# One transfer for w_out, paired quarters of w3, a bounded load queue and a new order in a fused attention and FFN kernel

## The chip, the cores and the metric

The kernel runs on one core of one Trainium2 chip. The core has five engines with an instruction queue each: PE (TensorE, matmuls and their weight loads), DVE (VectorE), ACT (ScalarE), POOL (GpSimd) and SP (SyncE, which here only issues transfers), and 16 DMA engines that they share. The metric is device time in microseconds (us), the median of several runs.

## The reference

The first part is linear attention with a polynomial sketch, in 4 batches of 4 heads with 1088 rows of 32; the second a multiplicative FFN on 4352 tokens of 128. q, k and v are float32. S1, S2 (8×32) and the FFN's weights arrive as float64.

```python
phi(x) = einsum(S1 x, S2 x) -> 64 features per row      # a_i * b_j
kv  = einsum('bhsf,bhsd->bhfd', phi(k), v);  z = sum(phi(k), over s)
num = einsum('bhsf,bhfd->bhsd', phi(q), kv)
den = einsum('bhsf,bhf->bhs', phi(q), z) + 1e-6
x   = (num / den) as (B*S, H*D) = (4352, 128)
a, b = x @ w1, x @ w2                                    # 128 x 1024 each
out = ((a * b) @ w3) @ w_out                             # 1024 x 1024, 1024 x 128
```

## The kernel before

**Weights.** float64 words come in as raw 8-byte integers and are made float32 on the chip. There are eleven chunks of 1 MB, `w0` to `w10`: w0 and w1 are the two column halves of w1 and w2, `w2` is the matrix w_out, `w3` to `w10` are eight blocks of 128 rows of the matrix w3. (A step's name `w3` is a chunk, not the matrix.) Chunk n has the steps `.load` (SP issues its transfers, L306 to L315), `.load2` (ACT's queue issues the rest, L328), `.c`, `.m` and `.s` (three passes on ACT, L343, L351, L347) and `.j`, `.a` (two on DVE, L362, L367). The buffer `raw` exists three times. Chunks 2 to 10 are loaded in quarters of 32 partitions (L317 to L324): quarters 0 and 2 from SP, 1 and 3 from ACT's queue. A chunk of w3 puts a quarter of the columns on each group of 32 partitions, four row blocks side by side.

**Fold.** w3 and w_out are multiplied beforehand into w3o. For block ko, `f{ko}.t` (L395) transposes the 32×32 squares of the chunk on DVE, `f{ko}.m` (L401) does eight matmuls against `wo`, and `f{ko}.o` (L405) copies the result to `w3o` on ACT. The partition on which a row of w_out lies fixes the order in which the transposes have to read the chunk.

**Attention.** Steps `k{b}.…`, `kr{m}.…`, `v{b}.…` and `kh{b}.…` load k and v and build the products with phi(k) for batch b. `.max`, `.lead`, `.rest` and `.l16` split k in parts, `.gram` (L516) multiplies them on PE, `.Gm` to `.Gb`, `.Ta`, `.Na` shape the results on DVE, `.kT`, `.ab`, `.abt` and `.kp` form phi(k), `.kv0` to `.kv3` and `.kvr` (L616, L623) multiply with v, `.kvm` (L630) masks them, `.kz`, `.ky` and `.kw` hold what q needs. Steps `q0` to `q7` take 512 rows of each of four heads, `qr` the 256 remaining tokens. `q0.A0`, `q0.C0`, `q0.A1`, `q0.C1` are its sketch matmuls, `.al`, `.phi` and the steps beginning with `s` make its features on DVE, `.pt0` and `.pt1` transpose them on PE (L1079), `.x` (L1098) multiplies with kv, `.xs` (L1104) divides on DVE, `.xT` copies the FFN's input on ACT. From q2 on the division is in `.pv` (L1072) and the input is made by `.xT0` to `.xT3` (L1140).

**FFN.** There are nine token groups, `g0` to `g7` with 512 columns and `gr` with 256. For each of eight column blocks c of the weights, `a` (L1182) and `b` (L1192) are matmuls into one of three PSUM buffers `h`, `c` (L1187) copies a on ACT, `m` (L1198) multiplies on DVE, and `o` (L1206; L1210 for gr) adds the product with w3o to the output. `.oT` transposes the output on DVE (L1219) and `.st` stores it by SP.

**Order.** Every piece of work is a named step. One list, ORDER (L36 to L95), names them all in the order in which they are put down, and the end of the kernel ties each instruction to the one before it on its engine (L1255 to L1259). So each engine does its steps in the order of that list, and a step that waits holds all that come later on its engine, transfers on SP included. The steps `warm0` to `warm9` are matmuls on zeros whose result isn't used (L181); WARM gives how many each does, 32 in all.

Of the kernel before, what the change touches and what calls it, by code (L numbers as in the profile page):

```python
# [25 lines left out]
WARM = [11, 3, 2, 5, 1, 1, 4, 1, 2, 2]  # L26

BY_PE = ()
QUEUE2 = "act"

# [6 lines left out]
c.zeros c.ident k0.zero k0.load0 k0.loadr k0.load1 v0.zero q0.load s.zero c.act s.load w0.load w1.load k0.max0  # L37
k0.max1 k0.nat0 k0.nat1 k0.g0 k0.g1 k0.lead0 warm0 k0.tr1 k0.lead1 k0.l160 k0.rest0 s.words k0.tr0 k0.rest1
k0.kT1 k0.gram0 k0.l161 s.pair q0.tr s.split k0.gram1 q1.tr s.lead w0.c s.P k0.Gm q0.restT k0.Gt q0.max k0.kT0
k1.zero k1.loadr k1.load kr0.load k0.Gr c.mask s.T w0.m w0.j k0.Ga s.blk kh1.load s.Pp q0.l2 warm1 k0.ab1 q0.l1  # L40
k0.abc1 v0.loadr k0.Gb warm2 k0.T0 w0.s q0.rm k0.kp1a k0.T1 k0.ab0 v0.load k0.Ta w3.load w1.c k1.max w2.load
k0.kp1b w3.load2 s.blkh k0.Tb warm3 q0.A0 q0.C0 k1.g w1.s w0.a k1.lead k0.N0 k0.Ts q0.sma k1.rest warm4 k0.N1
k1.kT1 kr0.tr kr0.kT k0.abc0 q0.sta warm5 kr0.ab q1.max k1.l16 k0.Na w1.m q0.sha warm6 k1.gram0 k0.kp0a k0.Nb
q0.sla k1.gram1 k1.kT0 w2.load2 k0.Nf k0.Nl k0.Nh warm7 q0.C1 w1.j kr0.abc q1.l2 kr0.kp q0.A1 q0.sca k0.kv0
q0.C1t w3.c k0.kv3 q0.smy q0.al k0.kv2 k0.kp0b q0.sty k1.gram2 q0.phi q1.l1 k2.zero k2.loadr warm8 k0.kv1 q1.rm
k2.load k0.kvr q0.pt0 w4.load w4.load2 q0.shy q0.pt1 k0.kvm q0.pc0 q0.sly k0.kzt k1.Gm kr1.load q0.scy k1.ab
q0.pc1 q0.p01 q0.p2 k0.kz w2.c k0.kw q0.p12 q1.A0 w1.a q0.x q1.load w2.m q0.dn k1.abt q1.C0 w2.s q0.de q1.sm
k1.kp1 q0.rc k1.Gt q0.xs w3.s k2.max q0.xt k0.kyt q0.xT q1.st k0.ky warm9 g0.0a w2.j w3.m w3.j g0.0b k2.g g0.0c
w2.a g0.3a w4.c g0.0m kr1.tr g0.1a g0.3c q1.sh kr1.kT k2.lead g0.3b g0.1c w4.s w4.j g0.1b k2.rest g0.3m g0.2a
q1.sl g0.1m g0.2b k1.Ga q1.scy k1.Gr g0.6a v1.zero v1.load v1.loadr w6.load w5.load w5.load2 g0.2c k2.l16 q1.sca  # L50
k1.Gb g0.5a w4.m g0.2m w3.a kr1.ab g0.5b g0.6c w7.load kr1.abc w4.a g0.5c k2.gram0 w7.load2 k2.gram1 q1.al g0.5m
k1.T0 w6.load2 k2.gram2 f0.t k1.T1 g0.6b k3.zero k3.loadr w5.m k1.kp0 kh2.load g0.7a g0.6m w5.c f1.t g0.4a g0.7c
k3.load f0.m q1.p01 g0.4c q1.p2 w5.s k2.Gm q1.p12 k1.Ta q1.dn g0.7b f0.o w5.j w6.c f1.m k1.Tb q1.de w5.a w7.c
q1.rc g0.0o g0.7m f1.o w6.m k1.Ts q1.bs g0.4b w6.j q1.phi w7.s g0.1o w10.load k1.kv0 w8.load f2.t w6.s k1.kv2
k1.kv1 k1.kv3 k1.kvr q1.pt0 w7.j w8.load2 q1.pt1 w6.a f2.m q1.pc0 q1.pc1 k1.kw f3.t w7.m q1.x g0.4m f2.o
w10.load2 w9.load f3.m w7.a q1.xT w8.c q2.tr k3.max g1.1a f3.o w8.m k1.N0 g1.1b k2.Gt f4.t g1.1c g0.3o w10.c
k2.kT1 k1.N1 g1.7a g1.1m q2.max g1.7b g1.7c k1.Na w9.load2 f4.m g1.7m w8.s w8.j k1.Nb g1.5a w10.j q2.l2 k1.Nf
f4.o w8.a g1.5b q2.l1 g1.5c g1.4a k1.Nl g1.5m k1.kyt f5.t g1.4c g1.4b w10.s g1.6a g1.4m g1.0a k1.ky k2.Gr g1.6c
k3.g k2.Ga k3.lead w9.m g1.6b k2.kT0 f5.m k3.l16 k1.Nh q2.rm k2.Gb w10.m k3.rest k2.ab g1.0c q2.C0 k2.abt w9.c
w10.a k2.kp0 k3.gram0 q2.A0 q3.tr k3.gram1 q1.restT k2.T0 k2.T1 g1.0b g1.6m k2.Ta g0.4o q3.max kr1.kp g0.2o  # L60
g1.0m k2.kp1 q3.l2 f7.t f5.o g1.2a q3.l1 w9.s g1.3a q2.At k2.Tb v2.zero v2.load q2.load kh3.load v2.loadr g1.2b
q3.rm g1.3c q2.Ct g1.2c k2.kv0 w9.j k3.gram2 q4.tr k2.kv1 k2.kv2 q3.C0 w9.a k2.Ts q2.sm k2.kv3 q3.A0 f6.t k2.kvr
f7.m v3.zero q2.st q4.max f6.m k3.Gm q4.l2 k3.kT0 f7.o g1.2m q4.l1 k2.kw q2.sh g0.5o k3.kT1 f6.o k2.N0 k2.N1
g0.6o k2.Na q2.sl g0.7o k2.Nb q2.scy q2.sca g1.3b g0.oT q2.al k3.ab g0.st q2.p01 q2.p2 g1.3m g1.0o q2.p12 k3.Gt
q2.dn g1.6o q3.At q2.de k3.Gr v3.load g1.4o q2.rc k3.Ga q2.bs k3.abt g1.1o q2.phi v3.loadr g1.3o q3.Ct k2.kyt
g1.2o q2.pv k2.ky g1.5o k3.Gb q4.rm q2.x k3.kp0 g1.7o q2.xT0 q2.xT3 q2.xT2 q3.sm q2.xT1 g2.2a q3.st q5.tr g2.2b
k3.kp1 g2.2c g2.0a g2.2m g2.7a q3.sh g2.0c q3.sl g2.0b g1.oT g2.7c q3.sca g1.st g2.7b q3.scy q3.al g2.0m g2.3b
k2.Nf q3.p01 q5.max g2.3a k2.Nh g2.7m k3.kv0 g2.3c q3.p2 k3.kv1 k2.Nl k3.kv3 g2.3m q4.A0 k3.kv2 q4.C0 q3.p12
q4.At q3.dn q3.de q5.l2 k3.kvr q3.rc g2.0o q3.bs q3.phi g2.1a q2.restT g2.6a q3.pv q3.load g2.1c q5.l1 g2.6b
k3.kw g2.6c g2.2o g2.6m q4.Ct g2.1b q5.rm q3.x q3.restT q4.sm q4.st g2.6o q3.xT0 q4.sh q3.xT3 g2.1m g2.5a g2.5b  # L70
g2.5c q3.xT2 q3.xT1 g2.1o g2.5m q5.A0 q5.C0 k3.T0 k3.T1 g3.5a k3.Ta k3.Tb g2.5o g3.5c k3.Ts q4.sl g3.5b qr.max
q5.At q5.sm g2.4a g3.5m g2.4b q4.scy g2.4c g3.0a g2.4m q4.sca g3.6a q7.tr q6.tr g2.3o g3.6c g3.0c g3.2a g3.6b
g3.0b g3.6m q4.al g2.4o g3.2c q4.p01 g3.0m qr.l2 g3.4a qr.l1 qr.rm g2.7o g3.4c k3.N0 g2.oT k3.N1 g3.2b q4.p2
g2.st g3.4b g3.2m q6.max g3.3a k3.Na g3.3b g3.3c q4.p12 q5.st q4.dn g3.0o q4.de q4.rc g3.4m g3.6o g3.3m g3.1b
q4.bs q4.phi g3.3o g3.1a k3.Nb k3.Nl q5.Ct g3.7a q4.pv k3.kyt g3.7c g3.2o k3.ky g3.1c q4.x g3.1m g3.5o q5.sh
q4.xT0 q4.xT3 q4.xT2 q5.sl q4.xT1 k3.Nh q5.scy g4.2a k3.Nf q5.sca g3.7b qr.A0 g3.7m qr.C0 q5.p01 g4.2b g4.2c
qr.At q5.al q6.l2 qr.sm q5.p2 g3.4o q5.p12 q5.dn g4.0a g4.2m g4.0b g4.0c g4.1a g4.0m qr.st g4.7a g4.1c q6.l1
g4.1b g4.7c g3.1o g4.1m q6.rm g4.3a q5.de q5.rc g4.7b g4.3c q5.bs q5.phi g4.5a g3.7o q5.pv g4.5b qr.Ct qr.sh
g4.7m q5.x q7.max g4.3b q5.xT0 q5.xT3 q5.xT1 g4.5c q6.A0 q5.xT2 q6.C0 g4.5m qr.sl g4.3m g5.0a qr.sca qr.al
qr.scy qr.p01 q6.At g4.4a g5.0c q6.sm qr.p2 g5.0b g3.oT g4.4c qr.p12 q7.l2 q6.st g3.st g4.0o g5.0m q7.l1 g4.4b  # L80
g4.6a g4.4m qr.dn g5.4a qr.de qr.rc q6.sh g4.5o g5.4c q6.sl qr.bs g4.6c q6.Ct g4.3o q7.rm g5.4b qr.phi g5.6a
g5.4m q6.sca g4.1o g5.6c g5.6b g4.4o g5.6m q6.scy g4.6b g5.5a g4.6m q6.al g5.5b q6.p01 g5.5c q6.p2 q6.p12 g5.1a
q6.dn qr.pv g5.3a q6.de q6.rc g5.5m qr.x g5.3c g5.1c g5.3b g5.7a g5.3m q6.bs g4.2o g5.7c q6.phi qr.xT0 qr.xT2
g4.6o qr.xT1 q7.C0 q7.A0 g4.7o q7.Ct g5.1b g4.oT q7.At g5.2a g4.st q7.sm g5.2b q7.st g5.1m g5.0o q6.pv g5.2c
qr.xT3 g5.4o q7.sh q6.x q7.sl g5.2m q7.scy g5.7b q7.sca q6.xT0 q6.xT3 q6.xT1 q6.xT2 g5.2o g5.7m q7.p01 g5.3o
q7.al q7.p2 g6.7a q7.p12 q7.dn g6.4a g6.7c g5.1o g6.4c g6.7b g6.4b g6.7m g5.6o g6.4m g6.6a g6.2a g6.6c g6.2b
g6.2c g6.6b g6.2m q7.de g6.3a g6.6m q7.rc g6.3b g6.3c q7.bs g6.5a g6.3m q7.phi g5.5o g6.0a q7.pv g5.7o g6.0c
g6.5c g6.5b g6.0b q7.x g6.0m g5.oT gr.3a q7.xT0 q7.xT2 g6.5m g5.st g6.0o gr.3c q7.xT3 q7.xT1 g6.1a g6.1b g6.1c
gr.3b g6.1m g7.0a gr.3m g6.2o g7.0c g7.1b g7.1a g6.6o g7.1c g7.1m g6.3o g7.0b g7.7b g7.0m g7.7a g6.4o g7.7c
g7.7m g6.5o g6.1o g7.4a g6.7o g7.4c g7.5a g6.oT g7.4b g6.st g7.5c g7.0o g7.4m g7.5b g7.2a g7.5m g7.2b g7.2c  # L90
g7.3a g7.2m g7.1o g7.3c g7.6b g7.6a g7.3b g7.6c g7.6m g7.4o g7.3m gr.5a gr.5b gr.5c g7.2o gr.5m gr.4a gr.4b
gr.4c g7.5o gr.4m gr.2a g7.3o gr.2c gr.2b g7.6o gr.2m g7.7o gr.0a g7.oT gr.0b gr.0c gr.1a g7.st gr.0m gr.7a
gr.1c gr.0o gr.7c gr.1b gr.3o gr.1m gr.2o gr.6b gr.6a gr.4o gr.6c gr.7b gr.6m gr.5o gr.7m gr.1o gr.6o gr.7o
gr.oT gr.st
"""  # L95


def bview(t, free):
    return bass.AP(tensor=t.tensor, offset=t.offset, ap=[list(t.ap[0])] + [list(d) for d in free])


def make_steps(ctx, tc, q, k, v, S1, S2, moe_w1, moe_w2, moe_w3, moe_w_out, out):
    nc = tc.nc
    dve, act, pe, pool, sp = nc.vector, nc.scalar, nc.tensor, nc.gpsimd, nc.sync
    B, H, S, D = q.shape
# [196 lines left out]
    def conv(n):  # L302
# [3 lines left out]
        def _():  # L306
            raw[n] = sb("raw", [128, 1024], I64)
            if n < 2:
                for i, w in enumerate((moe_w1, moe_w2)):
                    sp.dma_start(raw[n][:, i * 512:(i + 1) * 512], w[:, n * 512:(n + 1) * 512])  # L310
            elif n - 3 in BY_PE:
                sp.dma_start(raw[n], moe_w3[(n - 3) * 128:(n - 2) * 128])
            else:
                quarter(sp, 0)
# [975 lines left out]
```

## Time and profile before

| | |
|---|---|
| median of 5 runs | 276.0 us (273.41 to 276.7) |
| profiled execution | 276.1 us, span 274.3 us |
| granted TensorE clock, mean | 0.994 |
| PE busy | 256.3 us, 93% |
| DVE busy | 187.5 us, 68% |
| ACT busy | 110.8 us, 40% |
| POOL busy | 27.1 us, 10% |
| DMA | 22.52 MB, mean 82 GB/s |

Times inside the profile count from the start of the span; the execution's own time is 1.8 us longer. "L516" is line 516 of the kernel. PE's busy time overlaps its weight loads (PEld), and the rows of a timeline overlap too, since an instruction begins before the one ahead has left the pipeline. In a row of a group stand the line, the engine, the operation, what it writes and reads with the shape, how often, the busy us and mean ns of one, and the idle time of the engine just before. A wait is put down to what came last. "issue" is time in which an engine waited for nothing that the profile shows. The chain of work that ended last is followed back from the last instruction.

### The profile page before, as it was taken

Reading aid. Unit: us, or ns where it says so; the run is one execution under the profiler, and the core shown is the slowest. Engines: PE = TensorE matmul, PEld = TensorE weight load, DVE = VectorE, ACT = ScalarE, POOL = GpSimd, SP = SyncE. Lnnn points to the kernel's source line nnn. Section 1 sums busy time; section 2 is a strip of 40 time slices with the busy share of each in tenths; the row PEclk is TensorE's granted clock in tenths of the full one; section 3 lists DMA queues with packets and bytes.
Section 4 is the critical chain, followed back from the end, with each engine's and each line's share of the span. In section 5 each row is a group of like instructions: output and inputs, shape, how many; then the busy total and the mean of one; then the engine's idle time right before and its main releaser. Section 6 shows DMA issues by size and latency. Waiting matters only on the chain.

```text
span 274.3 us, 5772 instructions
## 1 busy us (share of the span) xinstructions
PE 256.3 (93%) x2341; PEld 140.7 (51%) x2341; DVE 187.5 (68%) x434; ACT 110.8 (40%) x192; POOL 27.1 (10%) x51
## 2 busy tenths in 40 slices
PE   8787399997979989999999999999999999999994
PEld 3574185574643758445454444444454444444574
DVE  4788389996959997999945786687658555223321
ACT  4765269768469652023322313334132123212121
POOL 2637022320000430000000000000000000000000
PEclk9999889999999999999999999999999999999999
DMA  7789879799982050502200200002002001102020
GB/s 210 266 217 235 180 187 246 174 229 202 221 162 70 9 160 2 110 12 41 84 1 1 38 2 2 0 2 38 0 2 39 2 0 19 20 2 38 0 37 21
DMA packets 32170, 22.52 MB, mean 82 GB/s; under 512 B 21392, under 2 KB 26640, under 8 KB 32144
## 3 DMA queue, kind: packets, MB, share of 16 engines
q1 hardware_dynamic: 28752, 16.92, 26.8%
q10 hardware_dynamic: 3392, 5.24, 8.7%
q8 instruction: 18, 0.29, 0.5%
q14 instruction: 8, 0.07, 0.1%
HBM read 19.93 MB, written 2.23 MB: 81 GB/s over the span
## 4 chain that ended last, share of the span: by engine, by line
PE 72%; DMA 11%; ACT 6%; DVE 3%; issue 3%; SPq 2%; POOL 1%; ACTq 1%; DVEq 0%
PE a_ps L1182 20%; PE ps_o L1206 20%; PE b_ps L1192 19%; DMA raw<-in_moe_w_dram 6%; DMA kh<-in_k_dram 3%; PE ps_c L862 3%; PE ps_xb L1126 2%; PE ps_w3o L401 2%; ACT sg L347 2%; ACT sg L351 2%; PE ps_o L1210 1%; PE ps_kv L616 1%; DMA kk<-in_k_dram 1%; PE ps_g L516 1%; ACT cv_c L343 1%
## 5 line engine op out<-in xcount | busy, mean ns | idle before, releaser
L1198 DVE TENSOR_TENSOR ab<-ffa,b_ps 128x512 f32<-128x512 f32 (+1 forms) x72 | 46.6, 650 | 53.5 <-PE b_ps L1192 35.8
L1187 ACT COPY ffa<-a_ps 128x512 f32<-128x512 f32 (+1 forms) x72 | 39.9, 561 | 95.7 <-PE a_ps L1182 83.3
L1192 PE MATMUL b_ps<-xT,w 128*128 128x512 f32 (+1 forms) x144 | 69.4, 574 | 0.0
L1182 PE MATMUL a_ps<-xT,w 128*128 128x512 f32 (+1 forms) x144 | 68.5, 575 | 0.4 <-ACT ffa L1187 0.3
L1206 PE MATMUL ps_o<-ab,w3o 128*128 128x512 f32 x128 | 63.8, 600 | 3.1 <-ACT w3o L405 3.1
L1182 PEld LDWEIGHTS a_ps<-xT,w 128*128 128x128 f32 x144 | 26.4, 190 | 31.6 <-issue 24.6
L1192 PEld LDWEIGHTS b_ps<-xT,w 128*128 128x128 f32 x144 | 26.2, 190 | 27.2 <-issue 22.6
L1206 PEld LDWEIGHTS ps_o<-ab,w3o 128*128 128x128 f32 x128 | 23.1, 190 | 28.5 <-issue 21.2
L401 PEld LDWEIGHTS ps_w3o<-wo,w3T 128*128 128x128 f32 x128 | 15.2, 192 | 2.9 <-issue 1.4
L343 ACT ACTIVATE cv_c<-raw 128x1024 f32<-128x1024 f32 x11 | 12.5, 1144 | 8.1 <-DMA raw<-in_moe_w_dram 8.1
L401 PE MATMUL ps_w3o<-wo,w3T 128*128 128x128 f32 x128 | 15.6, 277 | 0.0
L351 ACT ACTIVATE sg<-raw 128x1024 uint16<-128x1024 uint32 x11 | 15.1, 1375 | 1.0 <-DVE s_al L1020 1.0
L347 ACT CAST sg<-cv_c 128x1024 f16<-128x1024 f32 x11 | 14.5, 1348 | 0.0
L539 POOL TENSOR_TENSOR kp<-kabt 128x1024 f32<-128x1024 f32 x4 | 8.7, 2174 | 41.9 <-DVE kabt L598 36.2
L516 PE MATMUL ps_g<-kl 128*32 128x32 bf16 x144 | 7.9, 183 | 4.9 <-issue 4.7
L181 PE MATMUL idle_ps<-zeros 128*128 128x512 bf16 x32 | 11.2, 476 | 1.1 <-DVE zeros L156 1.1
L1140 ACT COPY xT<-ps_xb 128x128 f32<-128x128 f32 (+1 forms) x28 | 5.8, 281 | 13.8 <-PE ps_xb L1126 13.8
L839 ACT ACTIVATE q<-qT,q_m 128x512 f32<-128x512 f32 x8 | 5.7, 718 | 12.5 <-DVE G_g L145 4.6
L367 DVE CUSTOM_DVE_ANT_0 w3c<-w3c,sg 128x2048 uint16<-128x2048 uint16 x8 | 9.6, 1207 | 1.1 <-ACT sg L347 1.1
L516 PEld LDWEIGHTS ps_g<-kk 128*32 128x32 f32 x288 | 7.1, 114 | 5.5 <-issue 4.8
L395 DVE STREAM_TRANSPOSE w3T<-w3c 128x1024 f32<-128x1024 f32 x8 | 9.9, 1233 | 0.0
L1219 DVE STREAM_TRANSPOSE oT<-ps_o 128x512 f32<-128x512 f32 x8 | 5.7, 713 | 5.6 <-PE ps_o L1206 5.5
(214 smaller groups left out, 310.7 us busy)
## 6 DMA issues: line engine op xcount, KB each, us to landing
raw<-in_moe_w_dram ACTq DMA_DIRECT2D x16, 256.0 KB, 5.8
raw<-in_moe_w_dram SPq DMA_DIRECT2D x16, 256.0 KB, 6.1
qh<-in_q_dram SPq DMA_DIRECT2D x4, 544.0 KB, 4.3
raw<-in_moe_w_dram SPq DMA_DIRECT2D x4, 512.0 KB, 7.3
out_dram<-oT SPq DMA_DIRECT2D x32, 64.0 KB, 2.0
kk<-in_k_dram SPq DMA_DIRECT2D x3, 512.0 KB, 5.4
kh<-in_k_dram SPq DMA_DIRECT2D x12, 128.0 KB, 5.6
v<-in_v_dram SPq DMA_DIRECT2D x12, 128.0 KB, 5.2
```

The costliest lines, as they stand in the source:

```text
L181: pe.matmul(t, zeros[:, :128], bview(zeros, [[0, 2], [1, 256]]), start=True, stop=True)
L343: act.mul(shape(x["c"], 1, True), words(1).bitcast(F32), 2.0 ** -112)
L347: act.copy(bview(sign_bits[n % 2].bitcast(F16)[:, 1:], [[2, 1024]]), x["c"])
L351: act.mul(shape(sign_bits[n % 2].bitcast(U16), 2, True), words(0).bitcast(U32), 2.0 ** -29)
L395: dve.transpose(w3T[ko].rearrange("p s (i r) -> p s i r", r=32), bview(w3c[ko], [[32, NC], [256, 4], [1, 32]]))
L401: pe.matmul(t["o"], w3T[ko][:, c], wo[:, c], start=c == 0, stop=c == NC - 1)
L516: pe.matmul(o[h * D:(h + 1) * D], lhs, rhs, start=start, stop=stop, skip_group_check=True)
L1182: pe.matmul(x["a"][:, :w], w_of(0, c), xT[g][:, c0:c0 + w], start=True, stop=True)
L1187: act.copy(x["s"][:, :w], x["a"][:, :w])
L1192: pe.matmul(x["b"][:, :w], w_of(1, c), xT[g][:, c0:c0 + w], start=True, stop=True)
L1198: dve.tensor_mul(ab_sb[g, c][:, c0:c0 + w], x["s"][:, :w], x["b"][:, :w])
L1206: pe.matmul(o_ps[g][:, :n], w3o[:, c], ab[:, :n], start=c == 0, stop=c == NC - 1)
```

## The change

The matrix w_out is loaded in one SP transfer of 1 MB, in which partition p gets rows 8p to 8p+7 in one piece of 8 KB; before it came in four quarters from two queues. Chunk s of `wo` then holds rows 8p+s, so the fold's transposes read w3's chunk with a step of 8 elements (32 bytes) instead of in runs of 32. Of each chunk of w3, SP loads quarters 0 and 1 (partitions 0 to 63) and ACT's queue 2 and 3 (64 to 127). The pieces of v and kh are issued in the order 0, 2, 1, 3. A new constant DEPTH = 4 makes each SP transfer, from the fifth on, wait for the landing of the one issued four before it; that holds for stores too. ORDER is a new list, and WARM has 25 in place of 32 matmuls. The steps `.s` and `.a` may be given to POOL, but the set of POOL's steps isn't changed.

```diff
-WARM = [11, 3, 2, 5, 1, 1, 4, 1, 2, 2]
+WARM = [12, 1, 1, 1, 2, 1, 3, 1, 1, 2]
+DEPTH = 4
...
+            elif n == 2:
+                sp.dma_start(raw[n], moe_w_out.rearrange("(p s) d -> p (s d)", s=NC))
...
                 quarter(sp, 0)
-                quarter(sp, 2)
+                quarter(sp, 1)
...
-                for t in (1, 3):
+                for t in (2, 3):
                     quarter({"pool": pool, "act": act, "sp": sp}[QUEUE2], t)
...
-                dve.transpose(w3T[ko].rearrange("p s (i r) -> p s i r", r=32), bview(w3c[ko], [[32, NC], [256, 4], [1, 32]]))
+                dve.transpose(w3T[ko].rearrange("p s (i r) -> p s i r", r=32), bview(w3c[ko], [[1, NC], [256, 4], [NC, 32]]))
...
-                for t in range(4):
+                for t in (0, 2, 1, 3):
                     sp.dma_start(bview(v_sb[b][t * 32:(t + 1) * 32], [[NK * D, H], [1, NJ * D]]),
...
-                for h in range(H):
+                for h in (0, 2, 1, 3):
                     sp.dma_start(k_by[b][h * 32:(h + 1) * 32],
...
+        if DEPTH and ins.engine == nc.sync.engine and type(ins).__name__ == "InstDMACopy":
+            if len(loads) >= DEPTH:
+                tc.add_manual_dep(ins, loads[-DEPTH].name, landed, reason="depth")
+            loads.append(ins)
```

The part of ORDER around the first x, before and after:

```diff
-k1.kT1 kr0.tr kr0.kT k0.abc0 q0.sta warm5 kr0.ab q1.max k1.l16 k0.Na w1.m q0.sha warm6 k1.gram0 k0.kp0a k0.Nb
-q0.sla k1.gram1 k1.kT0 w2.load2 k0.Nf k0.Nl k0.Nh warm7 q0.C1 w1.j kr0.abc q1.l2 kr0.kp q0.A1 q0.sca k0.kv0
-q0.C1t w3.c k0.kv3 q0.smy q0.al k0.kv2 k0.kp0b q0.sty k1.gram2 q0.phi q1.l1 k2.zero k2.loadr warm8 k0.kv1 q1.rm
-k2.load k0.kvr q0.pt0 w4.load w4.load2 q0.shy q0.pt1 k0.kvm q0.pc0 q0.sly k0.kzt k1.Gm kr1.load q0.scy k1.ab
-q0.pc1 q0.p01 q0.p2 k0.kz w2.c k0.kw q0.p12 q1.A0 w1.a q0.x q1.load w2.m q0.dn k1.abt q1.C0 w2.s q0.de q1.sm
-k1.kp1 q0.rc k1.Gt q0.xs w3.s k2.max q0.xt k0.kyt q0.xT q1.st k0.ky warm9 g0.0a w2.j w3.m w3.j g0.0b k2.g g0.0c
+k1.gram0 w3.load k0.Nb q1.tr kr0.kT k0.Nf k0.abc0 k0.Nh q0.sha w1.m k0.Nl k0.kp0a q1.max kr0.ab q0.A1 q0.C1
+q0.sla q0.smy q1.l2 k1.kT0 k0.kp0b w4.load k0.kv0 k0.kv2 w0.s q0.C1t q0.sty q0.sca warm7 k0.kv1 q0.shy q0.al
+k0.kv3 q0.sly kr0.abc q0.phi q1.l1 k1.ab kr0.kp w4.load2 k0.kvr q0.scy q0.pt0 q0.p01 q0.p2 q0.pt1 k0.kvm q0.pc0
+q0.p12 k0.kzt w0.j k1.gram1 k0.kz q0.pc1 q0.dn q0.x w3.load2 w0.a w2.c q0.de q0.rc k1.abt k1.gram2 w2.m q0.xs
+q1.A0 k2.zero k2.load q1.rm warm8 q0.xt k2.loadr q1.sm q0.xT w5.load w1.j w2.s warm9 g0.0a k1.Gm q1.st w2.j
```

## The prediction

> **What bounds the kernel now.** I read the stretches of the span first, then the waits, the chain, and last the rows that price an operation. The stretches (columns: from:to, us; then busy us and instructions of PE, weight load, DVE, ACT, POOL; granted clock, DMA share, GB/s):
>
> ```profile
> 0.00:43.00 43.00, 33.06 (x473) 22.33 (x473) 30.36 (x87) 25.18 (x37) 16.08 (x42) 0.96 0.85 221
> 43.00:60.00 17.00, 17.00 (x163) 9.46 (x164) 16.25 (x39) 14.23 (x20) 5.28 (x4) 1.00 0.97 204
> 60.00:83.00 23.00, 19.31 (x170) 12.77 (x169) 16.73 (x28) 14.33 (x18) 0.00 (x0) 1.00 0.95 201
> 83.00:118.00 35.00, 34.10 (x414) 20.45 (x414) 33.24 (x82) 15.93 (x25) 5.74 (x5) 1.00 0.27 64
> 118.00:262.00 144.00, 144.00 (x1075) 68.57 (x1074) 88.11 (x198) 39.23 (x89) 0.00 (x0) 1.00 0.09 16
> ```
>
> From 118 to 262 us PE has no gap, and its work there isn't changed. So the end moves by what the first 118 us gain or lose. There DVE is the fullest engine: 16.25 of 17.00, then 33.24 of 35.00. Before 43, the first matmul of the FFN (42.93), no engine is full: a chain runs from q0 and k0 to the first x. Between 60 and 83 both PE and DVE have holes while DMA is 0.95 busy.
>
> Waits (engine, line, what it waited for: us in total, times, longest) and one row of PE's timeline, then links of the chain (start, us, what):
>
> ```profile
> PE ps_g L516 <- issue: 4.7, 1, 4.7
> DVE kvm L630 <- PE ps_kv L623: 5.5, 1, 5.5
> ACT cv_c L343 <- DMA raw<-in_moe_w_dram: 8.1, 3, 3.5
> 32.70 0.21 PE L516 MATMUL ps_g<-kl 128*32 128x32 bf16 x3 [4.67 <-issue]
> ```
>
> ```profile
> 28.04 4.67 issue
> ...
> 52.71 6.65 DMA raw<-in_moe_w_dram
> ...
> 59.38 4.55 DMA kh<-in_k_dram
> ...
> 70.78 9.59 DMA raw<-in_moe_w_dram
> ```
>
> PE stands from 28.04 to 32.70 inside k1.gram2, for nothing the profile can name. One 16 KB packet of the instruction queue falls into that gap, so I take it for an instruction fetch. DVE's 5.5 us wait for kvm is its echo: k0.kv1 and k0.kvr stand behind k1.gram2 on PE. Later the chain passes three DMA links, raw weights and kh.
>
> **The new order, up to the first x.** The q0 path must end with xs on DVE (L1104, ends 40.89). From 4.1 to 40.9 DVE was busy 28.10 us and idle 8.7. Summing each step's own duration in the new list up to xs gives 28.86 us against 32.87: w1.j 0.68, w1.a 1.22, q1.rm 0.69, k0.kw 0.42, q1.sm 0.41, q0.restT 0.23, k1.Gm 0.18, k1.Gt 0.17 go behind it, 4.0 in all. (Rows overlap; 28.10/32.87 turns 28.86 into 24.7.) k1.gram2 goes behind q0.x, and k0.kv1, k0.kvr, q0.pt0, q0.pt1 go ahead of k1.gram1. By instruction count the same point of PE's stream now falls at about q0.pt0, which waits for phi anyway, that is for several us of DVE steps after q0.C1; a fetch can run beside them. So I drop the 5.5 us of DVE's echo. New waits: k1.gram0 stands behind kr0.tr, whose 32 KB load now comes after kh1 and v0 (about 1.5 us), and q0.x behind k1.gram1 and kzt (1.5): +3.0. Bounds: 0, and 5.5 if the stall lands fully on the path. xs ends at 4.1 + 24.7 + (8.7 − 5.5 + 3.0) = 35.0, 5.9 earlier; with 2.2 to the first matmul (40.89 to 42.93 before, rounded up) the FFN begins at 37.2, 5.7 earlier.
>
> Not all of it is gain. q1.C0 (1.9 us of PE, 39.8 to 41.6 before) and k0.ky (0.3) now run after that point: +2.2. PE's idle between 43 and 118 is 0 + 3.7 + 0.9 = 4.6; the faster w3 takes 2.5 of it. Sum on PE: −5.7 + 2.2 − 2.5 = **−6.0**. DVE tells the same: up to q2.pv, 117.8 before, its steps sum to 109.36 us against 109.93, so work is only permuted; idle of 17.45 becomes 17.45 − 5.5 + 3.0 − 3.0 (raw, kh) = 12.0, and 4.1 + 95.7 + 12.0 = 111.8, 6.0 earlier.
>
> **Transfers.** Rates in three stretches (same columns):
>
> ```profile
> 10.00:12.00 2.00, 1.03 (x30) 0.66 (x25) 1.24 (x6) 1.89 (x4) 1.84 (x5) 1.00 0.97 393
> 46.00:49.50 3.50, 3.50 (x9) 1.52 (x8) 3.23 (x8) 2.56 (x5) 2.58 (x1) 1.00 1.06 220
> 71.50:80.00 8.50, 7.25 (x34) 4.31 (x33) 6.94 (x11) 3.54 (x5) 0.00 (x0) 1.00 1.08 210
> ```
>
> The first holds w1 and w2 over all 128 partitions, the second quarters of 32 partitions from SP alone, the third quarters from both queues. w_out in one transfer over 128 partitions: 1.05 MB at 393 is 2.7 us where 205 gave 5.1; two SP and two ACT issues (0.31 to 0.46 each) go, one comes. It is needed by the fold only: −2.4 beside other work, nothing on the path. w3 is 8.4 MB: 38 us at 220, 21 at 393. Now SP has partitions 0 to 63 and ACT 64 to 127; if the two run together, the three raw links shrink. Bounds for that: 0, and the 4.6 us of PE idle. I take 2.5, since kh and the chain through ACT (cv_c 1.14, sg 1.38 and 1.35 us per chunk, eleven times) stay. The Trainium skill speaks against the pairing: "SBUF — State Buffer", section "Can I just issue two DMAs to hit both halves?", says that two transfers to two halves of the partitions share the same engines and serialize, 6% better than one. By it the 2.5 us stay lost and the sum would be −3.5.
>
> DEPTH adds a wait to each SP transfer from the fifth on, for the landing of the one four before. Behind the waiting issue stand only later transfers; who waits for these: k1.kT1 for kh1's last piece, kr0.tr, w2.c. Four quarters are 1.05 MB, 4.8 us at 220, against 6.1 from issue to landing, so the queue may run dry for about 1.3 us per landing at worst; below zero is possible too, since fewer packets wait ahead of an urgent one. I take 0 beyond the 3.0 above; the bounds are in the range. Warm matmuls: 7 fewer at 0.2 to 0.35 on an idle PE, nothing. The mask on POOL earlier: −0.5 of a DVE wait, in the noise. The helper that goes had no effect, and the POOL set is the same.
>
> **The strided transposes.** w_out in one contiguous transfer gives partition p rows 8p to 8p+7, so f0.t to f7.t (L395) must read w3c every 32 bytes instead of in runs. No row shows DVE doing that; the nearest (busy us, mean ns):
>
> ```profile
> L395 DVE STREAM_TRANSPOSE w3T<-w3c 128x1024 f32<-128x1024 f32 x8 | 9.9, 1233 | 0.0
> ...
> L1140 ACT COPY xT<-ps_xb 128x64 f32<-128x64 f32 x4 | 0.8, 296 | 0.0
> ...
> L714 DVE TENSOR_REDUCE G_z<-ps_g 128x32 f32<-128x64 f32 x4 | 0.7, 182 | 0.0
> L145 DVE TENSOR_REDUCE G_g<-ps_g 128x1 f32<-128x32 f32 x4 | 0.7, 181 | 1.0 <-PE ps_g L516 1.0
> ...
> L681 ACT COPY krab<-ps_krab 128x64 f32<-128x64 f32 x2 | 0.4, 208 | 0.0
> ```
>
> L1140 writes SBUF in 16-byte steps, L681 the same 64 elements in a run: +88 ns, 1.4 ns an element, +1.41 us for 1024. L714 reads PSUM in 128-byte steps and costs no more than L145's run: +0. One shares the memory with the changed read, the other the engine; I take the middle, +0.7 us each, 5.6 for eight, and keep 0 and 11.3. They stand where DVE is busy 89% of the time (68.15 of 76.9), so 5.0 reaches the end. The Trainium skill's "Vector Engine (DVE) Microarchitecture Reference", section "Measured stream behaviour on trn2", says that a port keeps its full rate only for runs of two adjacent words, 1.73 instead of 1.054 ns an element when one source hops; it adds a one-source case without loss. By it eight transposes cost an estimated 5.5 us, or nothing.
>
> **Sum.** The profiled execution took 276.1 us (span 274.3 and 1.8 around it), next to the median, 276.0. 276.1 − 6.0 + 5.0 = **275.1**.
>
> **Rivals.** (F) The strided read is free: 270.1. For it: L714; against it: L1140. (A) Slower: the strided read costs what ACT's write does, 11.3 × 0.89 = 10.0 on DVE in f0.t to f7.t: 280.1. It turns the change into a loss from 6.0/(8 × 0.89) = 0.84 us per transpose on. (B) The DMA part doesn't do what it says: SP issues its quarters well ahead of ACT, which has conversions in front of its own, so each half still lands alone at 220, raw waits stay (+2.5), and the depth limit adds one dry gap on the path (+1.0): 278.6 with the middle price. For it: at 71.5 to 80 two queues together reached 210, no more than one.
>
> **Chances.** Forecast 0.33 (272 to 278), F 0.30 (266 to 273), A 0.20 (278 to 283), B 0.17 (276 to 281). About 1% is what a measurement can tell from no change, 273.3 to 278.8. Faster by more: 0.28 of F and 0.08 of the forecast, with 0.01 of B, 0.37. Within: 0.02, 0.23, 0.03 of A and 0.08 of B, 0.36. Slower: 0.02, 0.17, 0.08, 0.27. The range leaves out a tenth at each end: 266.5 to 281.5.
>
> **What would show it.** L395's mean: 1233 is F, 1.9 us the forecast, 2.6 A. DVE's first xs ends near 35, the first a_ps near 37; no wait of PE for issue above 2 us and none of DVE for kvm. Between 45 and 80 the rate stands near 390 in the stretches with quarters from both queues, or near 220 (B). cv_c waits for raw fall from 8.1 to about 4. PE is gapless from some 112 to 117. It would be wrong if the stall lands on q0.pt0 in full (+4.7), if kr0's late load holds k1.gram0 for more than 1.5, or if PE has gaps after 118, which no step here explains.

## The result, and the profile after

| | before | after |
|---|---|---|
| median | 275.24 us (91 runs) | 273.48 us (49 runs) |
| ratio | | 0.996, 95% interval 0.9945 to 0.9975 |
| profiled execution | 276.1 us, span 274.3 | 273.82 us, span 272.0 |
| first a_ps begins | 42.93 us | 36.28 us |
| PE idle from there to 118 us | 4.6 us | 5.2 us |
| one transpose of the fold | 1233 ns | 2041 ns |

The change gains 0.4%, with an interval that stays clear of 1. The forecast was 275.1 us after 276.0, inside 1% of no change. The time got there by a path that is only half the predicted one, and the experiments show which half.

The first a_ps is the first matmul of the FFN. The stretches of after, cut at the same places as those of before (from:to, us; busy us and instructions of PE, weight load, DVE, ACT, POOL; clock, DMA share, GB/s):

```profile
0.00:43.00 43.00, 39.77 (x475) 27.87 (x476) 32.73 (x89) 27.96 (x41) 13.37 (x41) 0.84 0.83 225
43.00:60.00 17.00, 12.97 (x133) 6.81 (x135) 16.46 (x27) 11.06 (x15) 5.43 (x2) 1.00 0.77 163
60.00:83.00 23.00, 22.54 (x210) 15.57 (x199) 20.93 (x34) 17.70 (x24) 3.08 (x5) 0.93 0.81 193
83.00:118.00 35.00, 34.34 (x477) 20.71 (x476) 34.52 (x89) 12.94 (x24) 4.95 (x3) 1.00 0.35 85
118.00:262.00 144.00, 144.00 (x1016) 68.67 (x1015) 86.42 (x194) 40.66 (x90) 0.00 (x0) 1.00 0.09 16
```

From 118 on PE is full, as before. The hole between 60 and 83 is closed, but 4.03 us are missing between 43 and 60, and DVE is now nearly full all the way from 36 to 118. The granted clock was lower twice: 0.84 in the first stretch and 0.93 in the third.

The waits of after (what waited, for what: us, times, longest), the first a_ps (start, busy; the wait in brackets) and the piece of its chain between 51 and 59 us (start, us, what):

```profile
PE ps_krt L662 <- DMA kr<-in_k_dram: 3.7, 1, 3.7
ACT cv_c L336 <- DMA raw<-in_moe_w_dram: 0.5, 1, 0.5
```

```profile
36.28 1.98 PE L1178 MATMUL a_ps<-xT,w 128*128 128x512 f32 x4 [0.24 <-ACT xT L1112]
```

```profile
51.27 3.61 DMA raw<-in_moe_w_dram
...
54.89 0.02 SPq L474
...
54.94 4.03 DMA kr<-in_k_dram
...
59.10 0.30 PE ps_krt L662
```

ACT's waits for raw weights, 8.1 us before, are 0.5. PE's stall of 4.67 us and DVE's wait of 5.5 us for kvm don't occur. What is new is kr1: 64 KB in two transfers of 32 KB. SP issued the second at 54.91, when a quarter of w3 had landed, and PE stood 3.7 us for it.

### The profile page after: what moved, and what is told of

Same layout as the page of the kernel before. It is cut to its first block, busy times and chain, and to the rows that moved or that the text cites. A ratio compares the mean times of both kernels' runs of the same rounds, so it can differ in the third digit from the quotient of the medians.

```text
span 272.0 us, 5765 instructions
## 1 busy us (share of the span) xinstructions
PE 260.1 (96%) x2334; PEld 145.6 (54%) x2334; DVE 193.3 (71%) x434; ACT 111.8 (41%) x192; POOL 26.8 (10%) x51
## 3 DMA queue, kind: packets, MB, share of 16 engines
q1 hardware_dynamic: 28352, 17.44, 25.7%
## 4 chain that ended last, share of the span: by engine, by line
PE 74%; DVE 15%; DMA 4%; issue 3%; ACT 2%; POOL 1%; DVEq 0%; POOLq 0%; SPq 0%
PE ps_o L1202 19%; PE a_ps L1178 18%; PE b_ps L1188 18%; PE ps_w3o L397 4%; DVE w3T L391 3%; PE ps_xb L1122 2%; DVE w3c L364 2%; PE ps_c L858 2%; DVE ab L1194 2%; DMA kr<-in_k_dram 1%; DVE k_g L146 1%; DMA raw<-in_moe_w_dram 1%; PE ps_o L1206 1%; PE ps_ab L560 1%; DMA kk<-in_k_dram 1%
## 5 line engine op out<-in xcount | busy, mean ns | idle before, releaser
L1188 PE MATMUL b_ps<-xT,w 128*128 128x512 f32 (+1 forms) x144 | 68.5, 572 | 0.0
L397 PEld LDWEIGHTS ps_w3o<-wo,w3T 128*128 128x128 f32 x128 | 16.4, 209 | 5.8 <-DVE w3T L391 3.5
L397 PE MATMUL ps_w3o<-wo,w3T 128*128 128x128 f32 x128 | 17.7, 297 | 1.5 <-DVE w3T L391 1.0
L391 DVE STREAM_TRANSPOSE w3T<-w3c 128x1024 f32<-128x1024 f32 x8 | 16.3, 2041 | 0.0
L336 ACT ACTIVATE cv_c<-raw 128x1024 f32<-128x1024 f32 x11 | 12.7, 1152 | 1.0 <-DMA raw<-in_moe_w_dram 0.5
L835 ACT ACTIVATE q<-qT,q_m 128x512 f32<-128x512 f32 x8 | 5.8, 723 | 12.7 <-PE ps_c L858 7.3
L1136 ACT COPY xT<-ps_xb 128x128 f32<-128x128 f32 (+1 forms) x28 | 5.6, 281 | 12.9 <-PE ps_xb L1122 12.7
L1057 DVE TENSOR_TENSOR ph<-s_al,s_bs 128x1024 f32<-128x1024 f32 (+1 forms) x8 | 9.2, 1150 | 0.1
L961 DVE STREAM_TRANSPOSE ay_A<-ps_a 128x256 f32<-128x256 f32 (+1 forms) x7 | 3.0, 427 | 8.1 <-PE ps_a L858 8.1
```

Of the source, the lines that this page charges most:

```text
L336: act.mul(x["c"], words(1).bitcast(F32), 2.0 ** -112)
L391: dve.transpose(w3T[ko].rearrange("p s (i r) -> p s i r", r=32), bview(w3c[ko], [[1, NC], [256, 4], [NC, 32]]))
L397: pe.matmul(t["o"], w3T[ko][:, c], wo[:, c], start=c == 0, stop=c == NC - 1)
L1188: pe.matmul(x["b"][:, :w], w_of(1, c), xT[g][:, c0:c0 + w], start=True, stop=True)
```

## The experiments

Each run is compared with before on its own chip; the difference of two ratios taken on different chips is uncertain by about 0.005, some 1.4 us. After itself is at 0.996.

**The stride of the transposes.**

```diff
-bview(w3c[ko], [[1, NC], [256, 4], [NC, 32]])
+bview(w3c[ko], [[32, NC], [256, 4], [1, 32]])
```

> The kernel after, but f0.t to f7.t read w3's chunk in runs of 32 again; w_out stays in one transfer, so the pairing of w3's columns with w_out's rows is left out and only the time is meant. Theory P (the stride is paid on the path): L391 falls from 2041 to about 1233 ns, 6.5 us less on DVE, and with 0.89 of it reaching the end the time falls by 5.0 to 6.5 us, to about 267 to 268.5. Rival H (DVE's extra time is hidden, the time is set by transfers and PE): L391 falls as much, the time by less than 2 us.

0.986 (0.981 to 0.991), 271.5 us. The group of the transposes in after and in this kernel (busy us, mean ns):

```profile
L391 DVE STREAM_TRANSPOSE w3T<-w3c 128x1024 f32<-128x1024 f32 x8 | 16.3, 2041 | 0.0
```

```profile
L391 DVE STREAM_TRANSPOSE w3T<-w3c 128x1024 f32<-128x1024 f32 x8 | 9.9, 1239 | 0.0
```

DVE loses 6.4 us of work, and the median falls by 2.0 to 2.8 us. Neither theory has its number: the stride is paid, but by less than half. Rival H's bound of 2 us lies within the uncertainty. The last stretch before PE's full one shows where:

```profile
83.00:118.00 35.00, 35.00 (x480) 21.30 (x479) 33.91 (x87) 13.70 (x26) 4.95 (x3) 1.00 0.37 100
```

With DVE relieved, PE has no gap left there (35.00 of 35.00). It could win back only the idle time it had: 5.2 us in after, of which the 3.6 us for kr1 aren't DVE's doing and stay. Between 43 and 118 the idle time fell from 5.15 to 3.79 us. That is 1.4 us; the rest of the 2.0 to 2.8 lies within the uncertainty, and no wait in the profile accounts for it.

**The limit on SP's queue.**

```diff
-DEPTH = 4
+DEPTH = 0
```

> The kernel after without the limit on SP's transfers (DEPTH = 0), all else the same. In the profile of after PE waits 3.7 us for kr1, whose load SP issued only when a quarter of w3 had landed. Theory W (the limit adds a wait on the path): that wait goes below 1 us, kr1.tr starts 3 us earlier, and the time falls by 1 to 3 us. Rival N (DVE is the bound there, PE's wait is covered): the wait goes, the time stays within 0.7 us. Rival G (the limit helps urgent loads past the bulk): kh, v and kr land later than 2.5 to 3.0 us, and the time rises by 1 us or more.

0.990 (0.986 to 0.994), 272.6 us: 0.9 to 1.8 us faster, not much more than the uncertainty, and not by theory W. PE still waits 3.6 us for kr1, since SP's second issue for it comes late without the limit too: it stands behind two quarters and goes out at 52.53 us, when a quarter has landed. Why it waits for that without the limit isn't shown. kh landed in 4.8 us in place of 2.5, as theory G says, and the time fell all the same; v (2.8 and 3.0 us) and kr (4.0 both) landed alike. So the limit makes kh faster, and nothing in after waits for it. Which wait the limit lengthens on the path isn't settled by this run.

**The pairing of quarters.**

```diff
-quarter(sp, 1)
+quarter(sp, 2)
...
-for t in (2, 3):
+for t in (1, 3):
```

> The kernel after, with SP taking quarters 0 and 2 of each chunk of w3 and ACT's queue 1 and 3, as before. Theory S (the two queues don't run together, or share one limit): landing of the quarters and the rate in the stretches with both queues stay within 10%, the time within 0.7 us. Rival C (halves of the partitions add up): the rate of after in such stretches is well above that of this kernel, and this kernel is slower by 1 to 3 us.

0.990 (0.986 to 0.993), 272.5 us. The old quarters are no slower, rather 1 to 1.7 us faster, and land sooner (SP 4.9 us, ACT's queue 5.2, in after 5.2 and 6.2). Theory C falls; theory S, which allowed 10% and 0.7 us, isn't met to the letter either. Two stretches of after show that the halves don't add up: from 53.5 to 57 only packets of ACT's quarters move (kr1's second transfer is issued in it, and none of its packets moves yet), from 73 to 76 quarters of both queues (last columns: clock, DMA share, GB/s).

```profile
73.00:76.00 3.00, 2.54 (x11) 0.90 (x11) 3.00 (x5) 2.74 (x4) 0.80 (x2) 1.00 1.08 213
53.50:57.00 3.50, 1.92 (x39) 0.77 (x38) 3.50 (x4) 1.20 (x1) 0.00 (x0) 1.00 1.09 207
```

213 GB/s with both, 207 with one. Whole-width transfers had 393 in before (10 to 12 us: w1 and w2, and k from 10.84 on). So quarters on the two halves of the partitions together move no more than quarters on one half alone.

**More filler ahead of the clock's fall.**

```diff
-WARM = [12, 1, 1, 1, 2, 1, 3, 1, 1, 2]
+WARM = [12, 1, 4, 1, 2, 1, 3, 1, 1, 2]
```

> The kernel after with warm2 of 4 matmuls in place of 1, ahead of the gap of PE near 11 us. In after the granted clock is 0.5 from about 12.7 to 25 us, where before had 1.00. Theory K (PE's thin work near 10 to 12 us lets the clock fall, and the chain to the first x runs at half speed): the clock stays at 1.00 from 12 to 24, the first a_ps starts 2 to 5 us earlier than 36.3, and the time falls by 1 to 4 us. Rival D (the clock falls for another reason, or DVE sets the chain): clock or time unchanged, or slower by up to 1 us for the filler itself.

0.994 (0.991 to 0.997), 274.0 us: no gain. PE's gap near 11.5 us shrank from 0.96 to 0.79 us only, and the clock was at 0.54 on average from 12 to 24. The test was too weak to decide, so it was repeated with 8, below.

**After again**, beside the next three.

> The kernel after, unchanged, on the chip and beside the runs of before that the next three share. Both theories: 0.996 of before, within 0.3%.

0.996 (0.993 to 0.9995), 274.0 us.

**kr1 earlier.**

```diff
-w7.load w3.s g0.1b kh2.load
+kr1.load w7.load w3.s g0.1b kh2.load
...
-g0.3m g0.2b k2.l16 f0.t w6.load g0.6b kr1.load g0.6c
+g0.3m g0.2b k2.l16 f0.t w6.load g0.6b g0.6c
```

> The kernel after with kr1.load moved ahead of w7.load in the order, and nothing else. In after PE waits 3.7 us for kr1 near 56 us, and PE's idle between the first a_ps and 118 us is 5.4 us in all. Theory E (the end is the first a_ps plus PE's work plus PE's idle, so every gap of PE there counts): the gap goes and the time falls by 2 to 3.6 us. Rival D (DVE, busy 34.5 of 35 us from 83 to 118, is the bound, and PE's gap is only its slack): the gap goes, another opens later, the time falls by less than 1 us.

0.986 (0.981 to 0.992), 271.8 us, 2.2 below after on the same chip. That is the lower end of theory E, and a wait did open in place of the gap: PE then stood 2.9 us in the fold for a conversion on ACT.

```profile
PE ps_w3o L397 <- ACT cv_c L336: 2.9, 1, 2.9
```

Not all of the 2.2 us need be kr1's doing. The mean clock of these runs is 0.984, that of after beside them 0.970. About 0.006 of it is the clock behind the old gap (0.93 from 60 to 83 in after, 1.00 here). The other 0.008 fits the first stretch (0.92 here and 0.84 in after), where the two kernels do the same work; by after's own scatter (last section, some 1.6 us for a difference of 0.02) it is worth an estimated 0.6 us. That leaves about 1.6 us, between theory E and rival D.

**The one transfer and its stride, put into before.**

```diff
+            elif n == 2:
+                sp.dma_start(raw[n], moe_w_out.rearrange("(p s) d -> p (s d)", s=NC))
...
-bview(w3c[ko], [[32, NC], [256, 4], [1, 32]])
+bview(w3c[ko], [[1, NC], [256, 4], [NC, 32]])
```

> The kernel before with w_out in one transfer and the strided transposes that this needs; order, quarters and warm matmuls as before. The transposes measure 2041 ns in after, 0.81 us more each, 6.5 us in all. Theory of the prediction (0.89 of it reaches the end): 5 to 6.5 us slower than before, about 281. Rival E (only what opens gaps of PE counts; taking the stride out of after gained some 2 to 3 us): 2 to 4 us slower. Rival F (PE's backlog covers it): within 1 us.

0.997 (0.9935 to 1.0006), 274.5 us, as rival F has it. The prediction's own step would have made this 5 us slower. The transposes did take 2058 ns. PE's stall and the first a_ps of this run (start, busy; the wait in brackets):

```profile
30.87 0.21 PE L518 MATMUL ps_g<-kl 128*32 128x32 bf16 x3 [3.19 <-issue]
```

```profile
39.63 1.12 PE L1184 MATMUL a_ps<-xT,w 128*128 128x512 f32 x2
```

The stall is 3.19 us instead of 4.67, DVE's wait for kvm 2.4 instead of 5.5, the first a_ps 3.3 us earlier than before. Later PE has 2.2 us of idle from 83 to 118, where before had 0.9; only 0.5 of it waited for DVE, 1.6 were waits for issue. In the fold PE waited 0.8 us for a transpose. So what the one transfer wins at the start may pay for a stride that costs PE about 1.3 us here.

**The same without the stride.**

```diff
-bview(w3c[ko], [[1, NC], [256, 4], [NC, 32]])
+bview(w3c[ko], [[32, NC], [256, 4], [1, 32]])
```

> The kernel before with w_out in one transfer, its transposes in runs of 32 as before (so the pairing of w3's columns with w_out's rows is left out). With the strided transposes as well the same kernel took 0.997 of before. Theory O (one transfer gains near the start, the stride takes it back): 1 to 3 us faster than with the stride, 0.985 to 0.993 of before. Rival F (in before's order PE has enough queued work that neither shows): within 0.3% of the kernel with the stride.

0.994 (0.990 to 0.998), 274.0 us on another chip. The stall was 1.98 us. So the one transfer by itself gains about 0.6%. That is just short of theory O's range and just inside rival F's. The two intervals overlap, and the stride's price in before's order, 0.8 us by the ratios, isn't resolved.

**A bridge over the gap of PE.**

```diff
-WARM = [12, 1, 1, 1, 2, 1, 3, 1, 1, 2]
+WARM = [12, 1, 8, 1, 2, 1, 3, 1, 1, 2]
```

> The kernel after with warm2 of 8 matmuls in place of 1, so that PE runs from 4.4 to 12.9 us without the gap of 0.96 us near 11.5; s.T's last two transposes wait until 11.9 anyway. With 4 the gap was 0.79 us and the clock still fell to 0.50 at 12.96. Theory K (that gap brings the clock down): the clock stays at 1.00 until 20 us or later, the first a_ps starts 1 to 2.5 us earlier than 36.3, the median falls by 1 to 2 us. Rival D (other thin stretches, or chance, decide): the clock falls between 12 and 15 us as before, the median stays within 0.7 us.

In this profile the clock and the first a_ps did as theory K says; the time didn't. From 12 to 24 us, in after, in this kernel and in the run with no limit, and below them PE's gap in after:

```profile
12.00:24.00 12.00, 12.00 (x61) 10.40 (x62) 6.25 (x20) 5.98 (x8) 3.74 (x4) 0.53 0.74 230
```

```profile
12.00:24.00 12.00, 9.88 (x110) 7.75 (x113) 9.33 (x32) 8.25 (x11) 6.13 (x5) 0.92 0.81 244
```

```profile
12.00:24.00 12.00, 9.54 (x102) 7.64 (x103) 9.54 (x31) 8.37 (x11) 6.46 (x6) 0.93 0.97 270
```

```profile
11.93 0.28 PE L266 MATMUL ps_s<-ident,sk_abs 8*128 8x8 f32 x2 [0.96 <-POOL sk_abs L252]
```

The clock stayed at 1.00 until 22 us, DVE got 9.33 us of work done in place of 6.25, and the first a_ps came at 35.26, 1.0 earlier. But it stayed at 1.00 until 22 us in the runs with no limit and with kr1 earlier too, and there the gap of 0.96 us was not filled. So this profile doesn't show that the gap brings the clock down. Over the runs something did change: none of these 12 has a mean clock below 0.974, where 30 of after's 50 are below 0.970. The median is 273.8 (0.995, 0.992 to 0.999), level with after. The gain went mostly into transfers: DVE's waits for k rose from 3.0 to 5.7 us, PE's for kr from 3.7 to 4.9 (the new part at 21.9, ahead of the first x), and PE's busy time from 43 to 60 us fell to 11.60.

```profile
DVE k_g L146 <- DMA kk<-in_k_dram: 5.7, 3, 2.9
PE ps_krt L662 <- DMA kr<-in_k_dram: 4.9, 2, 3.6
```

**The new order alone.** Before's code with after's ORDER and WARM (the step w2.load2 stands behind w2.load).

> The kernel before with after's list ORDER and its WARM alone: w_out in quarters from two queues, transposes in runs, quarters 0 and 2 on SP, no limit. Undoing each part of after by itself gave about -2.5 us (stride), -1.0 (limit), -1.3 (pairing). Theory A (the parts add): 0.980 to 0.987 of before, 270 to 271.5. Rival C (the parts undo the same gap, or the one transfer is needed at the start): 0.988 to 0.994, 272 to 273.5.

0.985 (0.981 to 0.990), 271.2 us, inside theory A's range. The order is worth 4 us, more than the whole change. The first a_ps was at 37.12, with a clock of 0.55 from 12 to 24. PE's idle time from there to 118 is 4.6 us, as in before, and the wait for kr1 is in it, without any limit; ACT's waits for raw weights are gone.

```profile
PE ps_krt L665 <- DMA kr<-in_k_dram: 3.1, 1, 3.1
```

The parts don't add in full, though. By the ratios this is 2.9 us below after, where undoing stride, limit and pairing one by one gave 2.5, 1.0 and 1.3. The run with the transposes in runs, which keeps limit, pairing and the one transfer, is level with it (0.986). So what these three cost together, as long as PE stands for kr1, isn't resolved.

**The new order, and kr1 earlier.** The same, with the move of kr1.load above.

> The kernel of the run before this with kr1.load moved ahead of w7.load. Theory E (a gap of PE behind the first a_ps counts in full): 1.5 to 3 us faster than that kernel, 268 to 270. Rival D (another wait opens in its place): within 0.7 us of it.

0.970 (0.966 to 0.975), **266.9 us**: the best version here, 4.4 us below the one before it, on the same chip, and more than theory E gave. It has none of the change's transfers.

```profile
43.00:60.00 17.00, 17.00 (x183) 10.80 (x182) 16.79 (x37) 15.38 (x20) 7.70 (x5) 1.00 0.75 177
60.00:83.00 23.00, 22.55 (x173) 13.99 (x172) 21.41 (x39) 17.42 (x24) 0.83 (x2) 1.00 0.86 203
83.00:118.00 35.00, 35.00 (x468) 20.42 (x467) 33.04 (x84) 13.11 (x25) 4.95 (x3) 1.00 0.36 89
```

PE idles 0.45 us from 43 to 118, where after had 5.15, and its clock is 1.00 throughout that time. Moving kr1 gave 2.2 us in after and 4.4 here. The transposes alone aren't what held it back: with transposes in runs, but limit and pairing kept, it gave 1.7 (the run with transposes in runs against the next one, which also has w_out in quarters; by the ratios).

**After, with transposes in runs and kr1 earlier.** w_out in quarters, as SP 0 and 1 and ACT's queue 2 and 3; limit and pairing kept.

> The kernel after with w_out in quarters (0 and 1 from SP, 2 and 3 from ACT's queue), so that the transposes read in runs, and kr1.load ahead of w7.load; paired quarters and limit kept. Theory A (the parts add): 2.5 + 2 us faster than after, near 269.5, and 1 to 2.5 us slower than the run with old quarters and no limit. Rival C (the same gap is mended twice): 270.5 to 272, level with that run.

0.980 (0.975 to 0.984), 269.6 us: by the ratios 2.6 us slower than the run before it. Theory A has both of its numbers within 0.2 us. Limit and pairing (with the order of the pieces of v and kh) together cost about 1% here, where kr1 no longer stalls PE. In the profile PE stood 2.2 us at 65.8 for a conversion on ACT, and the clock was 0.93 from 60 to 83, where the run before it had 1.00.

## Why the prediction was right, and where it wasn't

**The first x.** xs was to end at 35.0 and ended at 34.90 (34.23 and 0.67 us); the first a_ps was to begin at 37.2 and began at 36.28. The stall at q0.pt0 didn't come, and DVE's wait for kvm went, as the step says. But the number is partly luck. The prediction reckoned with nothing for the clock ("Warm matmuls: 7 fewer …, nothing"). In after it fell to 0.50 at 12.7 us, up to 26, and DVE was busy 6.25 of 12 us while PE worked at half speed. That the fewer warm matmuls did this isn't shown. The same work took its first a_ps to 35.35 in the run with kr1 earlier, where the clock kept to 1.00 until 22, and to 37.06 in the second run of after, where it fell at about 12.3.

**PE's idle behind it.** This is the step that failed: "the faster w3 takes 2.5 of it". The idle time was to fall from 4.6 to 2.1 us and rose to 5.2. The raw waits did go, but kr1 came into their place, 3.7 us, and the clock after that gap ran at about 0.6 from 60 to 64. The prediction read the new order for k0's and q0's steps and didn't follow SP's own list: kr1.load stands behind w6.load, whose buffer is freed only by a conversion. The wait belongs to the order, since the order alone has it too (3.1 us). Sum of PE: −6.65 at the start, +2.2 for q1.C0 and k0.ky, +0.6 of idle, and an estimated 1.6 for the 0.93 of 23 us at a lower clock, −2.2; the span moved by −2.3. Without the 2.5 the prediction's sum for the order is −5.7 + 2.2 = −3.5, and the order alone measured about −4 us: that part holds.

**The transposes.** The price was 0.7 us each and measured 0.81, between the two bounds (0 and 1.41); the middle was nearer than either end. "5.0 reaches the end", from DVE's 89%, was wrong: about 2.0 to 2.8 does in after, and before's order shows no loss that its interval resolves. DVE was full, and yet only PE's idle time could be won back. −6.0 and +5.0 were both too large, PE's gain by the gap for kr1 and the clock, the stride's price by what reaches the end, and the two errors nearly cancelled. That is why the forecast stood, and it is luck.

**The transfers.** "−2.4 beside other work, nothing on the path" for w_out was wrong: in before's order the one transfer moved the first a_ps from 42.93 to 39.63 and 40.79 in the two profiles, and the stall of PE from 4.67 to 3.19 and 1.98. That the one transfer makes an instruction fetch land sooner is a reading that fits: the 16 KB packet of the instruction queue moves at 29.7 us in before and at 28.2 and 27.9 in the two runs, and PE goes on 2.6 to 3.0 us after it each time. That the packet is PE's isn't shown. Rival B was right in its mechanism: both queues together reached 213 GB/s, one 207. It agrees with the rule of the Trainium skill that spoke against the pairing ("SBUF — State Buffer", section "Can I just issue two DMAs to hit both halves?"). Against a kernel without pairing and limit, B's price is its +1.0 for the limit alone, since its 2.5 is a gain that doesn't come. Measured so, the two cost an amount that isn't resolved beside kr1's gap, and 2.6 us without it. ACT's raw waits fell nevertheless, and they did so with the order alone.

**Rivals F and A.** F needed a free stride, and the trace has 2041 ns. A needed 0.84 us each to lose what the order gains. At 0.81 its condition was nearly met, and the loss didn't come, because the price isn't passed on in full (2.0 to 2.8 of 6.4 us).

## What to carry to other kernels

When one engine is saturated to the end, the time is the moment at which it starts plus its work plus its idle time after that. A cost on another engine reaches the end by the idle time that it makes there, however full that other engine is; so list the gaps of the saturated engine one by one, with what ended each, before pricing anything, and look at the clock behind each. Of a new order, follow each queue of transfers too: a load of 32 KB behind a bulk load that waits for its buffer cost about as much as eight slow transposes. And try the parts of a change one by one and together: here the order alone was worth 1.5%, with one load moved 3.0%, and the parts that came with it took most of that away. What a part costs depended on which gap was open: limit and pairing showed their 1% only once kr1's gap was closed.

## What the runs showed of the hardware

The granted clock fell to 0.50 for between 3 and 17 us near the start, at a different time in each kernel and run: from 12.7 to 26 us in after, from 13.2 to 30 with the order alone, from 22.3 to 25.7 without the limit, from 32.8 to 36 in before, behind the stall. Over 50 runs of after the mean clock lay between 0.960 and 0.986; the median time of those below 0.97 was 274.1 us, of those at 0.984 and above 272.5. So part of the scatter of this kernel, some 1.6 us, goes with the clock. Filling one gap of about 1 us raised the mean clock of the runs from 0.970 to 0.980. But with the same gap unfilled, the clock fell at 12.7 us in one profile and at 22.3 in another. What brings it on isn't shown.

A transpose on DVE that reads SBUF with a step of 32 bytes took 2041 ns in place of 1239 for 1024 elements a partition, +0.78 ns an element. This is a little over half of what ACT pays for writing with a step of 16 bytes (1.4 ns).
